# The second layer of a fused spectral filter and MLP as Strassen's seven products

## The chip, the cores and the metric

The kernel runs on one core of one Trainium2 chip. The metric is the time on the device in microseconds (us), the median of several runs. The core's engines work side by side, each in its own order: TensorE (PE, matmuls; its weight loads are shown as PEld), VectorE (DVE), ScalarE (ACT), GpSimd (POOL) and SyncE (SP, which here only starts DMAs). Matmul results land in PSUM; DVE and ACT carry them to SBUF.

## The reference

For 8 batches of 3008 tokens by 256 channels, a Fourier filter along the tokens, then two layers with a leaky ReLU between them over all 24064 tokens:

```python
X = np.fft.rfft(x, axis=1)
F = (filt_r + 1j * filt_i)[None, :, :]
y = np.fft.irfft(X * F, n=x.shape[1], axis=1)      # (8, 3008, 256)
h = y.reshape(24064, 256) @ w_in                   # 256 -> 2048
g = np.maximum(0.01 * h, h)
out = g @ w_out                                    # 2048 -> 256
```

Inputs and output are float32; the kernel works in float16 with float32 accumulation.

## The kernel before

**The two layers.** Tokens go in 47 chunks of 512 (CH). Time is cut into slots, eight to a chunk. In slot g of chunk ci, moe1_group (L397 to L415) computes layer one for two of the sixteen 128-wide blocks of the hidden dimension: four matmuls of 512 columns into one of two wide PSUM tiles (ph), then one ACT instruction that applies the leaky ReLU and writes 128x1024 float16 into the chunk's activation tile gts[ci]. In the same slot moe2_slice (L417 to L437) does an eighth of layer two of the chunk before: eight matmuls of 256 columns, with a 128x128 block of activations as the weights and a row block of w_out_sb as the moving operand. Two slots finish 128 tokens; ACT copies them from po_ps to an output buffer, and SP stores two such blocks at a time.

**The filter.** Each batch is filtered in two levels of a factored Fourier transform (94 x 32), as groups of matmuls with a turn through DRAM between them: s1_group (L195, 16 per batch), s2_group (L239, 12 per batch: two matmuls, then three DVE instructions L249 to L251 that multiply by the filter, and a POOL addition L253), sa_group (L257, 12 per batch), and sb_group (L267, 16 per batch), which writes the filtered tokens to yt. t1_load and t2_load bring the turned data back, x_load brings the next batch. Batch 0 is done ahead of the loop in another form. All groups take a PSUM tile from a ring of three (single, named pf) through bank(): a group's first matmul waits until the group three earlier has been copied out. The copies of s1_group and sa_group are ACT's (for batch 1 partly DVE's), those of sb_group are DVE's.

**The order.** The kernel writes its order by hand: every engine runs its instructions as the program lists them. plan() (L444) puts the groups of each batch into slots: for batch b from 2 on, 47b - 75 is the first slot of s1_group at 1.5 groups per slot, 47b - 60 that of s2_group with one every 2.5 slots, sa_group follows three slots later, and sb_group starts at 47b - 23 with 1.5 per slot. In a slot the order is layer one, then the planned groups, then the layer-two slice:

```python
    for slot in range(SL * (NCHUNK + 1)):
        ci, g = divmod(slot, SL)
        if ci < NCHUNK:
            moe1_group(ci, g)
        for f in tasks.get(slot, ()):
            f()
        if ci > 0:
            moe2_slice(ci - 1, g)
```

Of the kernel before, what the change touches and what calls it, by code (L numbers as in the profile page):

```python
# [10 lines left out]
P = 128  # L11
FP16 = mybir.dt.float16
FP32 = mybir.dt.float32
AL = mybir.AluOpType
# [58 lines left out]
def kernel(  # L73
# [9 lines left out]
    nc = tc.nc  # L83
    B, N, D = x.shape
    assert N == N1 * N2 and D == 256
    DFF = moe_w_in.shape[1]
    NCT = DFF // P
    NDT = D // P
    TOK = B * N
    CH = 512  # L90
    NCHUNK = TOK // CH
    assert NCHUNK * CH == TOK
    SL = 8

    f2_np, i1_np, small_np, f2t_np, i1t_np = _build_np_constants(N)
    f2_d = nc.inline_tensor(f2_np, name="fwd2_const")
# [10 lines left out]
    fb_sb = cpool.tile([P, NC, D], FP16, name="fb_sb")  # L107
    w_in_sb = cpool.tile([P, NDT, DFF], FP16, name="w_in_sb")
    w_out_sb = cpool.tile([P, NCT, D], FP16, name="w_out_sb")
    x_sb = cpool.tile([P, N2, D], FP16, name="x_sb")  # L110
    big = [cpool.tile([P, Q * D], FP16, name=f"big{i}") for i in range(3)]
    yt = cpool.tile([P, NDT, 2 * N], FP16, name="yt")
# [2 lines left out]
    drp = ctx.enter_context(tc.tile_pool(name="drp", bufs=1, space=bass.MemoryType.DRAM))  # L115
    scrp = ctx.enter_context(tc.tile_pool(name="scr", bufs=2))
    ypp = ctx.enter_context(tc.tile_pool(name="ypp", bufs=4))
    outp = ctx.enter_context(tc.tile_pool(name="outst", bufs=6))
    psp = ctx.enter_context(tc.tile_pool(name="psp", bufs=1, space=bass.MemoryType.PSUM))


    wide = [psp.tile([P, 2 * CH], FP32, name=f"ph{i}") for i in range(2)]
    single = [psp.tile([P, CH], FP32, name=f"pf{i}") for i in range(3)]
    po_ps = psp.tile([P, 2, D], FP32, name="po_ps")
    turn = {"ph": 0, "pf": 0}

# [44 lines left out]
    one = cpool.tile([1, 1], FP32, name="one")  # L171
# [6 lines left out]
    K4 = 4 * NC  # L178
# [16 lines left out]
    def s1_group(b, g, copy):  # L195
        def go():
            ps = bank("pf", 2, D)
            nc.tensor.matmul(ps, fwd1[:N1], x_sb[:N1, ds(2 * g, 2), :], start=True, stop=True)  # L198
            h = g // 2
            copy(st1[h % 4][:, ds(2 * (g % 2), 2), :], ps)  # L200
            if g % 2:
                nc.sync.dma_start(dz1[b % 2][ds(4 * h, 4)].rearrange("n p d -> p n d"), st1[h % 4])
        return go

    def t1_load(b, c):
        def go():
            nc.sync.dma_start(z1[c % 4], turned(dz1[b % 2], N2, c))
        return go

    def t2_load(b, h):  # L210
        def go():
            nc.sync.dma_start(z2[h % 4][:K4], turned(dz2[b % 2], NC, h))
        return go
# [25 lines left out]
    def s2_group(b, g):  # L239
        def go():  # L240
            ps = bank("pf", 2, D)
            for j in range(2):
                nc.tensor.matmul(ps[:, j, :], f2_sb[:, 2 * g + j, :],  # L243
                                 z1[g // 2 % 4][:, 2 * (g % 2) + j, :],
                                 start=True, stop=True)
# [3 lines left out]
            nc.vector.tensor_tensor(p1[:], ps, fa, AL.mult)  # L249
            nc.vector.scalar_tensor_tensor(p2[0:64], ps[64:P], -1.0, fb[64:P], AL.mult, AL.mult)  # L250
            nc.vector.tensor_tensor(p2[64:P], ps[0:64], fb[0:64], AL.mult)  # L251
            y1 = ypp.tile([P, 2, D], FP16, tag="y", name=f"y_b{b}_g{g}")
            nc.gpsimd.tensor_tensor(y1[:], p1[:], p2[:], AL.add)  # L253
            ys[(b, g)] = y1
        return go

    def sa_group(b, g):  # L257
        def go():
            ps = bank("pf", 2, D)
            nc.tensor.matmul(ps, inv2, ys.pop((b, g))[:], start=True, stop=True)  # L260
            h = g // 2
            nc.scalar.copy(st2[h % 4][:, ds(2 * (g % 2), 2), :], ps)  # L262
            if g % 2:
                nc.sync.dma_start(dz2[b % 2][ds(4 * h, 4)].rearrange("k p d -> p k d"), st2[h % 4])
        return go

    def sb_group(b, g, copy):  # L267
        h, dt = g // 2, g % 2

        def go():  # L270
            ps = bank("pf", 4, N1)
            for j in range(4):
                nc.tensor.matmul(ps[:, j, :], z2[h % 4][:K4, j, ts(dt, P)], i1_sb[:K4, 4 * h + j, :],  # L273
                                 start=True, stop=True)
# [6 lines left out]
    act, dve = nc.scalar.copy, nc.vector.tensor_copy  # L281
# [110 lines left out]
    nc.sync.dma_start(f2_sb[:], f2t_d.ap())  # L392


    gts, pos, osts = {}, {}, {}

    def moe1_group(ci, g):  # L397
# [16 lines left out]
                    )  # L414
        nc.scalar.activation(gts[ci][:, ds(2 * g, 2), :], ph, AF.Lrelu)  # L415

    def moe2_slice(ci, g):  # L417
        tj, half = g // 2, g % 2
        last = ci == NCHUNK - 1
        if last and half == 0:  # L420
            pos[ci] = bank("pf", 1, D)[:, 0, :]
        po = pos[ci] if last else po_ps[:, tj % 2, :]
        for ct in range(8 * half, 8 * half + 8):
            nc.tensor.matmul(po, gts[ci][:, ct, ts(tj, P)], w_out_sb[:, ct, :],  # L424
                             start=(ct == 0), stop=(ct == NCT - 1))
        if half == 0:
            return
        if tj % 2 == 0:
            osts[ci] = outp.tile([P, 2, D], FP32, tag="ost", name=f"ost_c{ci}_t{tj}")
        ost, t0 = osts[ci], ci * CH + tj * P  # L430
        nc.scalar.copy(ost[:, tj % 2, :], po)  # L431
        if last:
            nc.sync.dma_start(out[ds(t0, P), :], ost[:, tj % 2, :])
        elif tj % 2 == 1:
            nc.sync.dma_start(
                out[ds(t0 - P, 2 * P), :].rearrange("(j t) d -> t j d", t=P), ost[:])


    tasks = {}

    def at(slot, f):
        tasks.setdefault(int(slot), []).append(f)

    def plan(b, s1, per, s2, step, lag, sb, rate):  # L444
        for g in range(16):
            at(s1 + g / per, s1_group(b, g, dve if b == 1 and g % 4 < 3 else act))
            if g % 2 and b + 1 < B:
                at(s1 + g / per + 2, lambda n0=2 * g - 2: x_load(b + 1, n0, 4))
        for c in range(4):
            at(s2 - 3, t1_load(b, c))  # L450
        for g in range(12):
            at(s2 + step * g, s2_group(b, g))
            if g % 2 and g < 4:
                at(s2 + step * g, t1_load(b, 4 + g // 2))
            at(s2 + lag + step * g, sa_group(b, g))
        for h in range(4):
            at(sb - 3, t2_load(b, h))
        for g in range(16):
            at(sb + g / rate, sb_group(b, g, dve))
            if g % 2 and g < 8:  # L460
                at(sb + g / rate, t2_load(b, 4 + g // 2))

    at(9, lambda: nc.sync.dma_start(i1_sb[:K4], i1t_d.ap()))
    plan(1, 0, 2, 12.5, 1, 3, 31, 2)
    for b in range(2, B):
        z = 47 * b
        plan(b, z - 75, 1.5, z - 60, 2.5, 3, z - 23, 1.5)

    for slot in range(SL * (NCHUNK + 1)):
        ci, g = divmod(slot, SL)  # L470
        if ci < NCHUNK:
            moe1_group(ci, g)
        for f in tasks.get(slot, ()):
            f()
        if ci > 0:
            moe2_slice(ci - 1, g)


# [28 lines left out]
```

## Time and profile before

| | |
|---|---|
| Median of 3 runs | 795.32 us (793.85 to 796.42) |
| The profiled execution's own time | 793.45 us |
| Its span in the trace | 791.7 us |
| Granted TensorE clock, mean | 0.998 of full speed |
| DMA | 92.48 MB, mean 117 GB/s |
| Second layer: matmuls of 128x256 | 3008, in po_ps and (last chunk) pf |
| First layer: leaky ReLU instructions | 376, mean 1024 ns |

In the profile a group line names the source line, engine and operation, the output and input tiles, their shapes, and the count; then the busy time and the mean length of one instruction; then how long the engine stood idle just before instructions of the group, and which instruction ended that wait. A line in order of time begins with the start in us from the span's start and the length of a run of equal instructions; a bracket at its end gives the idle time before it and what released it. The chain that ended last is followed back from the last instruction, and gives each engine's share of it.

### The profile page before, as it was taken

The numbers are of one execution on the slowest core, as the hardware profiler recorded it, in microseconds if no ns is written. First come the engines' busy times: TensorE is split into PE (matmuls) and PEld (weight loads), VectorE is DVE, ScalarE is ACT, GpSimd is POOL, SyncE is SP. The second block draws the span as 40 slices with busy tenths as digits, with TensorE's granted clock in tenths as the row PEclk, the third lists the DMA queues.
The fourth block names the chain that finished last, engine by engine and source line by source line (L and its number), as shares of the span: only waits on it lengthen the run. The fifth ranks groups of instructions, "written<-read, shape, count | busy, mean of one in ns | idle before, by whom it ended". The sixth has DMA issues, their size and how long they took to land.

```text
span 791.7 us, 13770 instructions
## 1 busy us (share of the span) xinstructions
PE 772.6 (98%) x5685; PEld 521.8 (66%) x5685; DVE 267.3 (34%) x408; ACT 553.4 (70%) x785; POOL 158.5 (20%) x171
## 2 busy tenths in 40 slices
PE   9888989999999999999999999999999999999998
PEld 4545556666676666666668666666667767666666
DVE  5837416441344224441344403443144423100000
ACT  4766866678677786777766787677867766666664
POOL 5624402221122211222112222222002210000000
PEclk9999999999999999999999999999999999999999
DMA  9994693218731295224932169212642232001111
GB/s 189 243 248 139 152 236 106 67 55 196 203 94 54 69 235 162 67 67 118 240 114 76 54 148 243 85 58 67 178 138 84 67 94 82 34 34 41 41 41 54
DMA packets 105422, 92.48 MB, mean 117 GB/s; under 512 B 12096, under 2 KB 88512, under 8 KB 105168
## 3 DMA queue, kind: packets, MB, share of 16 engines
q1 hardware_dynamic: 90496, 75.13, 30.1%
q0 software_dynamic: 14864, 16.49, 13.8%
q8 instruction: 44, 0.72, 0.4%
q14 instruction: 18, 0.15, 0.1%
HBM read 57.48 MB, written 50.33 MB: 136 GB/s over the span
## 4 chain that ended last, share of the span: by engine, by line
PE 92%; DMA 3%; DVE 2%; ACT 2%; issue 0%; DVEq 0%; SPq 0%; ACTq 0%
PE po_ps L424 40%; PE ph L410 39%; PE pf L198 3%; PE pf L273 2%; PE pf L243 2%; DMA dz<-big 2%; PE pf L260 2%; DMA big<-dz 1%; PE po_ps L348 1%; PE pf L424 1%; PE pf L320 1%; PE ph L299 1%; DVE big L233 0%; ACT gt_c L415 0%; ACT big L262 0%
## 5 line engine op out<-in xcount | busy, mean ns | idle before, releaser
L415 ACT ACTIVATE gt_c<-ph 128x1024 f16<-128x1024 f32 x376 | 384.7, 1024 | 203.6 <-PE ph L410 202.8
L410 PE MATMUL ph<-yt,w_in_sb 128*128 128x512 f16 (+3 forms) x1600 | 386.4, 366 | 0.3 <-DVE yt L340 0.3
L424 PE MATMUL po_ps<-w_out_sb,gt_c 128*128 128x256 f16 x2944 | 381.5, 272 | 0.0
L424 PEld LDWEIGHTS <-gt_c 128*128 128x128 f16 x3008 | 291.6, 98 | 87.9 <-issue 8.2
L410 PEld LDWEIGHTS <-w_in_sb 128*128 128x128 f16 x1600 | 154.4, 98 | 100.8 <-issue 4.3
L253 POOL TENSOR_TENSOR y_b_g<-p_b_g,p_b_g 128x512 f16<-128x512 f32 x84 | 106.4, 1267 | 355.1 <-DVE p_b_g L251 354.2
L276 DVE CAST yt<-pf 128x376 f16<-128x376 f32 x112 | 58.0, 546 | 210.9 <-PE pf L273 210.8
L249 DVE TENSOR_TENSOR p_b_g<-pf,fa_sb 128x512 f32<-128x512 f32 x84 | 58.0, 691 | 179.2 <-PE pf L243 170.3
L431 ACT COPY ost_c_t<-po_ps 128x256 f32<-128x256 f32 x184 | 69.5, 377 | 8.6 <-PE po_ps L424 7.0
L250 DVE SCALAR_TENSOR_TENSOR p_b_g<-pf,fb_sb 64x512 f32<-64x512 f32 x84 | 58.2, 692 | 1.1
L200 ACT CAST big<-pf 128x512 f16<-128x512 f32 x100 | 55.8, 590 | 3.9 <-DMA dz<-big 3.9
L251 DVE TENSOR_TENSOR p_b_g<-pf,fb_sb 64x512 f32<-64x512 f32 x84 | 57.4, 683 | 1.1
L142 POOL DMA_DIRECT2D x_sb<-in_x_dram x62 | 31.9, 517 | 121.0 <-PE pf L198 120.2
L262 ACT CAST big<-pf 128x512 f16<-128x512 f32 x84 | 48.8, 581 | 0.3 <-PE pf L260 0.3
L198 PE MATMUL pf<-x_sb,small_sb 94*128 94x512 f16 x112 | 37.3, 379 | 5.0 <-DVE big L200 2.9
L273 PEld LDWEIGHTS <-big 96*128 96x128 f16 x448 | 27.7, 98 | 20.8 <-DMA big<-dz 3.6
L273 PE MATMUL pf<-i_sb,big 96*128 96x94 f16 x448 | 31.8, 206 | 3.1 <-DMA big<-dz 3.1
L243 PE MATMUL pf<-big,f_sb 128*128 128x256 f16 x168 | 32.1, 272 | 2.0 <-DMA big<-dz 1.8
L260 PE MATMUL pf<-y_b_g,small_sb 128*128 128x512 f16 x84 | 31.9, 379 | 0.6 <-DVE p_b_g L251 0.6
L243 PEld LDWEIGHTS <-f_sb 128*128 128x128 f16 x168 | 15.9, 98 | 19.5 <-issue 3.0
L348 PE MATMUL po_ps<-idle 128*128 128x512 f16 x49 | 14.8, 450 | 1.2 <-DVE one L172 1.2
L198 PEld LDWEIGHTS <-small_sb 94*128 94x128 f16 x112 | 10.4, 98 | 8.1 <-issue 0.4
(52 smaller groups left out, 142.6 us busy)
## 6 DMA issues: line engine op xcount, KB each, us to landing
dz<-big SPq DMA_DIRECT2D x98, 256.0 KB, 3.2
out_dram<-ost_c_t SPq DMA_DIRECT2D x92, 256.0 KB, 2.2
big<-dz SPq DMA_DIRECT2D x42, 256.0 KB, 3.4
big<-dz SPq DMA_DIRECT2D x56, 192.0 KB, 4.9
x_sb<-in_x_dram POOLq DMA_DIRECT2D x41, 192.0 KB, 5.4
x_sb<-in_x_dram POOLq DMA_DIRECT2D x2, 768.0 KB, 10.0
w_in_sb<-in_moe_w_in_dram POOLq DMA_DIRECT2D x1, 1024.0 KB, 14.2
w_out_sb<-in_moe_w_out_dram POOLq DMA_DIRECT2D x1, 1024.0 KB, 12.5
```

The source lines that it names most:

```text
L198: nc.tensor.matmul(ps, fwd1[:N1], x_sb[:N1, ds(2 * g, 2), :], start=True, stop=True)
L243: nc.tensor.matmul(ps[:, j, :], f2_sb[:, 2 * g + j, :], z1[g // 2 % 4][:, 2 * (g % 2) + j, :], start=True, stop=True)
L249: nc.vector.tensor_tensor(p1[:], ps, fa, AL.mult)
L250: nc.vector.scalar_tensor_tensor(p2[0:64], ps[64:P], -1.0, fb[64:P], AL.mult, AL.mult)
L251: nc.vector.tensor_tensor(p2[64:P], ps[0:64], fb[0:64], AL.mult)
L253: nc.gpsimd.tensor_tensor(y1[:], p1[:], p2[:], AL.add)
L273: nc.tensor.matmul(ps[:, j, :], z2[h % 4][:K4, j, ts(dt, P)], i1_sb[:K4, 4 * h + j, :], start=True, stop=True)
L276: copy(yv[:, :, ds(4 * h, 4)], ps.rearrange("p c a -> p a c"))
L410: nc.tensor.matmul(ph[:, j, ds(o, ln)], w_in_sb[:, dt, ts(ct, P)], yt[:, dt, ds(lo, ln)], start=(dt == 0), stop=(dt == NDT - 1),)
L415: nc.scalar.activation(gts[ci][:, ds(2 * g, 2), :], ph, AF.Lrelu)
L424: nc.tensor.matmul(po, gts[ci][:, ct, ts(tj, P)], w_out_sb[:, ct, :], start=(ct == 0), stop=(ct == NCT - 1))
L431: nc.scalar.copy(ost[:, tj % 2, :], po)
```

## The change

For 44 of the 47 chunks (2 to 45) layer two becomes Strassen's scheme in Winograd's form. The activations of a chunk are cut in quarters a11, a12, a21, a22 (256 tokens by 1024 hidden each, as the first index counts tokens), and so is w_out (b11 to b22, 1024 by 128). Seven products of quarters replace eight:

- four combinations of w_out's quarters are made once, on POOL (wt);
- for each chunk DVE makes four combinations of activation quarters, each 128x2048 float16: s1, then a21 in place, s2 and s4 (act_sums, one at the end of each of slots 0 to 3);
- a product is 16 matmuls of 128 columns: two token blocks t by eight hidden blocks c. A chunk has seven, 112 matmuls or 14 in each slot, in this order: 0: a11 b11; 1: s4 b22 of the chunk before; 2: a12 b21; 3: s2 wt[1]; 4: a21 wt[2]; 5: a22 wt[3]; 6: s1 wt[0]. Product p is items 16p to 16p + 15 of the chunk, so it ends in slot p + 1 (product 6 with slot 7), at item 2p + 1 of that slot;
- ACT copies product 0 to t1; every other product is added to a partial sum by DVE, product 6 to two, so that seven DVE instructions of 128x256 replace four ACT copies. The sums go to output buffers, or to u2, u3, u4, which lie in float32 in the tile big[0], as do s1, s2 and s4.

Products alternate between two PSUM tiles, po_ps and the third tile of the FFT ring. The ring of the planned groups keeps two tiles. Output buffers go from six to four.

The plan moves: x_load of batch 2 later by 7.5 slots, s1_group to 47b - 75.5, s2_group to 47b - 60.25 with one every 2.75 slots, sb_group to 47b - 22 at 1.25 per slot; the copies of sb_group are now ACT's (for batch 1 half and half); the load of i1_sb goes from slot 9 to 18. Chunks 0, 1 and 46 keep whole-width matmuls (plain), 16 to each 128 tokens, with ACT copies.

```diff
+    NCH = NCT // 2
+    W0 = 2
...
+    wt_sb = cpool.tile([P, 4, NCH, P], FP16, name="wt_sb")
...
-    outp = ctx.enter_context(tc.tile_pool(name="outst", bufs=6))
+    outp = ctx.enter_context(tc.tile_pool(name="outst", bufs=4))
...
+    psp_last = single[-1]
...
+    single.pop()
+    out_banks = [t[:].rearrange("p (a t d) -> p a t d", a=2, t=2)
+                 for t in (psp_last, po_ps.rearrange("p a d -> p (a d)"))]
...
-    def moe2_slice(ci, g):
...
+    b11, b12 = w_out_sb[:, :NCH, :P], w_out_sb[:, :NCH, P:]
+    b21, b22 = w_out_sb[:, NCH:, :P], w_out_sb[:, NCH:, P:]
+    wt = [wt_sb[:, i] for i in range(4)]
+    for o, i0, i1 in ((wt[0], b12, b11), (wt[1], b22, wt[0]), (wt[2], b22, b12), (wt[3], b21, wt[1])):
+        nc.gpsimd.tensor_tensor(o, i0, i1, AL.subtract)
+
+    TH = CH // 2
+    sums = big[0][:, : 3 * NCH * TH].rearrange("p (i c t) -> p i c t", i=3, c=NCH)
+    s1, s2, s4 = (sums[:, i] for i in range(3))
...
+    def quarter(ci, i, j):
+        return gts[ci][:, ts(j, NCH), ts(i, TH)]
+
+    def act_sums(ci, step):
+        a11, a12, a21, a22 = (quarter(ci, i, j) for i in range(2) for j in range(2))
+        o, i0, i1, op = ((s1, a21, a22, AL.add), (a21, a11, a21, AL.subtract),
+                         (s2, s1, a11, AL.subtract), (s4, a12, s2, AL.subtract))[step]
+        nc.vector.tensor_tensor(o, i0, i1, op)
...
+    def product(ci, a, w, after):
+
+        po = out_banks[done["products"] % 2][:, 0]
+        done["products"] += 1
+
+        def one(t, c):
+            nc.tensor.matmul(po[:, t], a[:, c, ts(t, P)], w[:, c, :],
+                             start=(c == 0), stop=(c == NCH - 1))
+            if t == 1 and c == NCH - 1:
+                after(po)
+        return [lambda t=t, c=c: one(t, c) for t in range(2) for c in range(NCH)]
...
+    def added(*sums):
+
+        def after(po):
+            for o, with_ in sums:
+                nc.vector.tensor_tensor(o() if callable(o) else o, po, with_, AL.add)
+        return after
+
+    def last_product(ci):
+        def after(po):
+            added((half(ci, 0, 1), u4))(po)
+            store(ci, 0)
+        return product(ci, s4, b22, after)
+
+    def products(ci):
+        a11, a12, a21, a22 = (quarter(ci, i, j) for i in range(2) for j in range(2))
+
+        def after5(po):
+            added((half(ci, 1, 1), u3), (u4, u2))(po)
+            store(ci, 1)
+
+        items = product(ci, a11, b11, lambda po: nc.scalar.copy(t1, po))
+        if ci > W0:
+            items += last_product(ci - 1)
+        else:
+            done["products"] += 1
+            items += [lambda: None] * (2 * NCH)
+        items += product(ci, a12, b21, added((lambda: half(ci, 0, 0), t1)))
+        items += product(ci, s2, wt[1], added((u2, t1)))
+        items += product(ci, a21, wt[2], added((u3, u2)))
+        items += product(ci, a22, wt[3], added((lambda: half(ci, 1, 0), u3)))
+        items += product(ci, s1, wt[0], after5)
+        return items
...
-                at(s1 + g / per + 2, lambda n0=2 * g - 2: x_load(b + 1, n0, 4))
+                at(s1 + g / per + (2 if b > 1 else 9.5), lambda n0=2 * g - 2: x_load(b + 1, n0, 4))
...
-            at(sb + g / rate, sb_group(b, g, dve))
+            at(sb + g / rate, sb_group(b, g, dve if b == 1 and g % 2 else act))
...
-    at(9, lambda: nc.sync.dma_start(i1_sb[:K4], i1t_d.ap()))
+    at(18, lambda: nc.sync.dma_start(i1_sb[:K4], i1t_d.ap()))
...
-        plan(b, z - 75, 1.5, z - 60, 2.5, 3, z - 23, 1.5)
+        plan(b, z - 75.5, 1.5, z - 60.25, 2.75, 3, z - 22, 1.25)
+
+    items = []
     for slot in range(SL * (NCHUNK + 1)):
         ci, g = divmod(slot, SL)
+        wino = W0 <= ci - 1 < NCHUNK - 1
+        if g == 0 and ci > 0:
+            items = products(ci - 1) if wino else plain(ci - 1)
+            if ci == NCHUNK:
+                items = last_product(ci - 2) + items
         if ci < NCHUNK:
             moe1_group(ci, g)
         for f in tasks.get(slot, ()):
             f()
-        if ci > 0:
-            moe2_slice(ci - 1, g)
+        for f in items[len(items) * g // SL : len(items) * (g + 1) // SL]:
+            f()
+        if wino and g < 4:
+            act_sums(ci - 1, g)
```

In the changed kernel the planned groups' matmuls stand at L202 (stage one), L247, L264 and L277, the POOL addition at L257, the products at L461, the DVE additions at L476 and the activation sums at L447.

More of the change, by code (lines that the diff above doesn't have):

```diff
@@ L415, in moe1_group @@
         nc.scalar.activation(gts[ci][:, ds(2 * g, 2), :], ph, AF.Lrelu)
-    def moe2_slice(ci, g):
-        tj, half = g // 2, g % 2
+    b11, b12 = w_out_sb[:, :NCH, :P], w_out_sb[:, :NCH, P:]
[5 more added lines that the diff above has]
+    sums = big[0][:, : 3 * NCH * TH].rearrange("p (i c t) -> p i c t", i=3, c=NCH)
@@ new lines @@
+    s1, s2, s4 = (sums[:, i] for i in range(3))
+    part = [big[0][:, 3 * NCH * TH :].bitcast(FP32)[:, ts(i, TH)].rearrange("p (t d) -> p t d", t=2)
+            for i in range(4)]
+    t1, u2, u3, u4 = part
+    def quarter(ci, i, j):
[5 more added lines that the diff above has]
+        nc.vector.tensor_tensor(o, i0, i1, op)
@@ new lines, with store @@
+    done = {"products": 0}
+    def store(ci, i):
+        t0 = ci * CH + i * TH
+        nc.sync.dma_start(out[ds(t0, TH), :].rearrange("(j t) d -> t j d", t=P), osts[ci, i][:])
+    def product(ci, a, w, after):
[7 more added lines that the diff above has]
+        return [lambda t=t, c=c: one(t, c) for t in range(2) for c in range(NCH)]
@@ new lines, in half @@
+    def half(ci, i, k):
+        if (ci, i) not in osts:
+            osts[ci, i] = outp.tile([P, 2, D], FP32, tag="ost", name=f"ost_c{ci}_h{i}")
+        return osts[ci, i][:, :, ts(k, P)]
+    def added(*sums):
[8 more added lines that the diff above has]
+        return product(ci, s4, b22, after)
@@ L419, in moe2_slice, with plain, one @@
+    def plain(ci):
         last = ci == NCHUNK - 1
[L420 to L423, printed above, removed]
+        def one(tj, ct):
+            po = out_banks[tj % 2].rearrange("p a t d -> p (a t d)")[:, :D]
             nc.tensor.matmul(po, gts[ci][:, ct, ts(tj, P)], w_out_sb[:, ct, :],
                              start=(ct == 0), stop=(ct == NCT - 1))
-        if half == 0:
-            return
@@ L428, in moe2_slice @@
[L428 to L436, printed above, removed]
+            if ct < NCT - 1:
+                return
+            i, j = divmod(tj, 2)
@@ L439 @@
+            if j == 0:
+                osts[ci, i] = outp.tile([P, 2, D], FP32, tag="ost", name=f"ost_c{ci}_h{i}")
+            nc.scalar.copy(osts[ci, i][:, j, :], po)
+            if last:
+                nc.sync.dma_start(out[ds(ci * CH + tj * P, P), :], osts[ci, i][:, j, :])
+            elif j == 1:
+                store(ci, i)
+        return [lambda tj=tj, ct=ct: one(tj, ct) for tj in range(4) for ct in range(NCT)]
     tasks = {}
```

## The prediction

> **What bounds the kernel now.** I read the shares of busy time first, then the chain that ended last, then the costliest groups, then the order of time inside single slots. Shares and chain:
>
> ```profile
> PE 772.6 (98%) x5685; PEld 521.8 (66%) x5685; DVE 267.3 (34%) x408; ACT 553.4 (70%) x785; POOL 158.5 (20%) x171
> PE 92%; DMA 3%; DVE 2%; ACT 2%; issue 0%; DVEq 0%; SPq 0%; ACTq 0%
> PE po_ps L424 40%; PE ph L410 39%; PE pf L198 3%; PE pf L273 2%; PE pf L243 2%; DMA dz<-big 2%; PE pf L260 2%; DMA big<-dz 1%; PE po_ps L348 1%; PE pf L424 1%; PE pf L320 1%; PE ph L299 1%; DVE big L233 0%; ACT gt_c L415 0%; ACT big L262 0%
> ```
>
> TensorE is the bound nearly everywhere, split evenly over the two layers. VectorE is idle two thirds of the time. The groups that give my durations:
>
> ```profile
> L415 ACT ACTIVATE gt_c<-ph 128x1024 f16<-128x1024 f32 x376 | 384.7, 1024 | 203.6 <-PE ph L410 202.8
> L424 PE MATMUL po_ps<-w_out_sb,gt_c 128*128 128x256 f16 x2944 | 381.5, 272 | 0.0
> L253 POOL TENSOR_TENSOR y_b_g<-p_b_g,p_b_g 128x512 f16<-128x512 f32 x84 | 106.4, 1267 | 355.1 <-DVE p_b_g L251 354.2
> L249 DVE TENSOR_TENSOR p_b_g<-pf,fa_sb 128x512 f32<-128x512 f32 x84 | 58.0, 691 | 179.2 <-PE pf L243 170.3
> ```
>
> [...] the pitch has to come from runs in order of time (start, length, engine, count):
>
> ```profile
> 400.40 0.34 PE L273 MATMUL pf<-i_sb,big 96*128 96x94 f16 x4
> 400.80 1.03 PE L424 MATMUL po_ps<-w_out_sb,gt_c 128*128 128x256 f16 x8
> ```
>
> Eight of 256 columns: (1.03 - 0.27)/7 = 109 ns each. Four of 94 columns, each with a fresh weight load: (0.34 - 0.206)/3 = 45 ns. A straight line through the two puts 128 columns at 58 ns; the 128-column pieces of L410 that stand where a chunk crosses the end of yt start 56 ns apart in the trace. I take 56.
>
> One slot with four FFT groups (PE alone), and a stage-two block with its neighbour on POOL:
>
> ```profile
> 88.51 1.03 PE L410 MATMUL ph<-yt,w_in_sb 128*128 128x512 f16 x4
> 89.37 0.38 PE L260 MATMUL pf<-y_b_g,small_sb 128*128 128x512 f16 x1
> 89.86 0.38 PE L243 MATMUL pf<-big,f_sb 128*128 128x256 f16 x2
> 90.08 0.38 PE L198 MATMUL pf<-x_sb,small_sb 94*128 94x512 f16 x1
> 91.12 0.38 PE L198 MATMUL pf<-x_sb,small_sb 94*128 94x512 f16 x1 [0.67 <-ACT big L262]
> 91.34 1.04 PE L424 MATMUL po_ps<-w_out_sb,gt_c 128*128 128x256 f16 x8
> 92.21 1.03 PE L410 MATMUL ph<-yt,w_in_sb 128*128 128x512 f16 x4
> ```
>
> ```profile
> 87.71 0.69 DVE L249 TENSOR_TENSOR p_b_g<-pf,fa_sb 128x512 f32<-128x512 f32 x1 [1.37 <-PE pf L243]
> 88.42 0.69 DVE L250 SCALAR_TENSOR_TENSOR p_b_g<-pf,fb_sb 64x512 f32<-64x512 f32 x1
> 89.12 0.68 DVE L251 TENSOR_TENSOR p_b_g<-pf,fb_sb 64x512 f32<-64x512 f32 x1
> 89.96 1.26 POOL L253 TENSOR_TENSOR y_b_g<-p_b_g,p_b_g 128x512 f16<-128x512 f32 x1 [1.72 <-DVE p_b_g L251]
> ```
>
> With three tiles in the ring the fourth group had to wait until ACT had copied the first, 2.61 us after the slot began (91.12 - 88.51): ACT must run the slot's leaky ReLU (1.02) before that copy (0.58). This slot lasted 3.70 us against 2.60 by its matmuls, 1.10 lost. And a stage-two group occupies DVE for 2.09 us in one piece.
>
> **What the skill says.** (1) The Trainium skill, "TensorE: Matmul & The Clock Gate", "Back-to-back issue gap": about 81 ns for a matmul of 128 columns in a stream of load and matmul pairs, 56 alone. The 45 ns above, with a load each, speak for 56. (2) "VectorE: DVE Perf Modes", "The perf-mode tier table": a tensor_tensor with all operands 16-bit in SBUF makes two results a cycle, 2048 elements in 1224 ns; in fp32 2293. No such instruction is in this trace. (3) "SBUF — State Buffer", "Who interferes with whom": a VectorE instruction with two SBUF inputs and a GpSimd instruction that reads SBUF lock each other out for a whole instruction. L249 to L251 take one input from PSUM and show no such thing.
>
> **The change, part by part.**
>
> *Matmuls.* 44 of 47 chunks change. Per chunk 64 x 109 = 6.98 us goes, 112 x 56 = 6.27 comes: 0.70 less, **-31.0 us** in all. This is the whole gain on offer.
>
> *ACT.* 176 output copies (0.377) go, 44 copies to t1 and 104 yt copies (about 0.5, as L340 on ACT) come: +2 us in sum, and 8 x 1.02 + 0.4 per chunk leaves slack. A t1 copy behind two stage-one copies is late by some 0.3; with about seven such places, **+2**.
>
> *DVE, sum.* Adds: L249 extrapolated to 256 columns is 0.42 (0.44 with the step between instructions), seven per chunk. Activation sums: 1.24 with that step by (2), four per chunk. About 7.9 us per chunk, 346 in all, less 57 of yt copies: 267 becomes about 556. Not a bound by its sum, so what counts is when.
>
> *DVE, order.* A product's PSUM tile is reused by the product after next, whose first matmul waits for the add. Product p ends in slot p+1 and product p+2 starts in slot p+2 at item 2(p+2): the add must be out within one product. A stage-two block ahead of it is in the way. Call the slot of a stage-two group k (within its chunk), time from its first L243. DVE frees at 0.48 + 2.09 = 2.57 (0.48: 89.86 to DVE's 90.34 in the slot above), the add is out at 3.07. PE gets to the next product at 0.22 (L243) + 0.78 (14 items) + 0.86 (layer one: 89.37 - 88.51) + 0.112(k+1) = 1.87 + 0.112(k+1).
>  - k=3: 3.07 - 2.31 = 0.76; k=4: 0.64; k=5: 0.53; k=6: none, since two layer-one groups lie between.
>  - k=2: the sum s2 is queued behind that add, and the fourth product needs it: 3.07 + 1.24 - 2.20 = 2.1.
>  - k=1: a sum, an add and s2's sum follow the block: 2.57 + 1.24 + 0.44 + 1.24 + 0.06 = 5.55 against 0.22 + 2 x (0.78 + 0.86) + 0.34 = 3.85: 1.7. k=0, one more sum and one more slot: 6.79 - 5.50 = 1.3. k=7, two adds first: 7.67 - 7.15 = 0.5.
>
> The new plan puts 72 groups into changed chunks, at k=0..7: 9, 8, 10, 8, 9, 10, 8, 10. Sum 11.6 + 13.6 + 20.9 + 6.1 + 5.8 + 5.3 + 0 + 5.2 = **+68.5**; about 3 less for groups that stand in the next slot and lengthen it. Nothing gives these waits back: PE takes its matmuls in order.
>
> *Lock between DVE and POOL.* If (3) holds, the sum of DVE that follows an add finds L253 (1.27) running: k=2 loses 0.96 more, k=1 0.83, k=0 0.9, k=3 0.6, k=7 0.5: 34 us in all. Without it 0. No trace shows it and POOL is often first only by 0.1 us; I take half, **+17**, and keep both ends.
>
> *Chunks without FFT work.* DVE: two adds, two sums, then the add of the second product (ready at 4.62 from the chunk's start), then s2's sum: out at 6.36, needed at 6.14. 0.2 in some 15 chunks, **+3**.
>
> *Two ring tiles instead of three.* Now the third group of a slot waits for the first one's copy: 2.61 after the slot's start, 2.54 if it is a yt copy, when PE would be there at 1.22 to 1.30. Price 1.3, the size of the 1.10 seen above. For batches 2 to 7 the new plan has 15 slots with three groups and 5 with four (1.6 each, the fourth waits 0.3 more): 27.5. For batch 1, six more at 1.3, and slots 19, 21, 23 lose 2.2 instead of 1.1: 11. Together **+38.5**. Slots with three groups cost nothing in the trace, with three tiles.
>
> *At nothing:* the four weight differences on POOL (4 x 2.5 by L253's rate; the first y_b_g comes some 20 us into the loop, POOL idles 355 us; without cover 10 us). Later x_loads (one batch ahead). Stores: same bytes, but they sit in SP's queue waiting for a late DVE, ahead of turned loads issued three slots (5.2 us) early that take 3.4 to 4.9: at most some 2 us in a few places. Fewer output buffers: four against at most three in use.
>
> Sum against the profiled execution: 793.45 - 31.0 + 68.5 - 3 + 17 + 38.5 + 3 + 2 = 888.5 (its span 791.7 and 1.75 around it, unchanged). The median of the runs is 1.9 higher, so **890 us**.
>
> **Rivals.**
>  - *The matmul saving wins* (faster): PE's waits for DVE do not form, because a block delays an add by less than PE's way to the next product. It decides at about 1.9 us from L243 to a free bank; I have 3.07 from measured rows. For it: DVE has two thirds of its time free. Then 793 - 31 + few = about 770.
>  - *Sums at one element a cycle*, 2.28 each: three stand before the fourth product, +3.1 in each of 44 chunks, +136: about 1025. For it: nothing but the absent row.
>  - *Weight loads set the pitch*, 81 ns: 112 x 81 = 9.07, +92 on PE instead of -31; longer slots shrink the DVE waits to about 40: about 965. Against: 45 ns at 94 columns.
>
> **How the numbers follow.** Forecast 0.80, its own range 845 to 925: down to no lock and two thirds of the ring waits (793 - 31 + 65 + 26 + 5 = 858, and some of the blocks half hidden), up to the full lock (907) and late loads. Saving wins 0.08, one element a cycle 0.07, 81 ns 0.05. The range for 8 in 10, 842 to 930, leaves the three out. About 0.3% is what a measurement tells from no change: faster 0.08, same 0.02 (a near cancelling), slower 0.90.
>
> **What would show it.** L461 at 56 ns a step in unbroken runs; the sums at about 1.22 us; DVE's share near 60%; idle time of PE ahead of L461, released by DVE (some 80 us), and ahead of L202, L247, L264 and L277, released by ACT (some 40); sums of DVE stretched beyond 1.22 beside L257 on POOL if the lock is real; and the last eight chunks, free of FFT, shorter than before. If PE shows few waits for DVE, the order argument is wrong; if L461 runs at 80 ns, the first term is.

## The result and the profile after

The changed kernel takes 901.29 us (897.17 to 904.96, 4 runs) against 794.60 us (793.85 to 796.42, 4 runs) for the one before on the same chip: a ratio of 1.134, 95% interval 1.128 to 1.140. The forecast was 890, with a range of 842 to 930. The profiled execution took 904.96 us, its span is 903.2 us, and the granted TensorE clock is 0.964 on average, where it was 0.998.

Shares of busy time, the clock in 40 slices, and the chain that ended last:

```profile
PE 782.4 (87%) x7797; PEld 539.3 (60%) x7797; DVE 578.0 (64%) x788; ACT 554.8 (61%) x757; POOL 184.2 (20%) x175
PEclk9999899899999999999999999999999989999999
PE 16%; DVE 1%; ACT 0%; issue 0%; DVEq 0%
```

VectorE is busy for 64%, where the forecast had near 60%, and no engine is full: TensorE fell from 98% to 87%. The clock dips in three slices, which it did in none before. The chain accounts for 17% of the span and breaks off there, so it is no help for this kernel; the waits have to do.

The waits of TensorE that other engines end (engine, line, what released it: us in total, times, longest; PEld's waits overlap PE's, so the two are not added):

```profile
PEld L461 <- DVE big L447: 60.0, 23, 4.7
PE po_ps L461 <- DVE big L447: 30.0, 12, 4.5
PE pf L461 <- DVE big L447: 26.1, 11, 4.5
PE pf L247 <- ACT yt L280: 11.1, 10, 1.2
PE pf L202 <- ACT yt L280: 8.8, 10, 1.1
PE pf L202 <- ACT big L266: 7.5, 7, 1.2
PE pf L277 <- DMA big<-dz: 7.2, 4, 2.6
PE po_ps L461 <- DVE big L476: 5.2, 12, 0.5
```

Two families are large. A product waits for an activation sum (L447), 56 us in 23 places; and a group with one of the two ring tiles waits for ACT's copy, in steps of about 1.1 us. The third forecast family, a product that waits for the addition that frees its tile (L476), is there too, but small in each place. In a few places a group waits for the turned data from DRAM (big<-dz).

The costliest groups concerned:

```profile
L257 POOL TENSOR_TENSOR y_b_g<-p_b_g,p_b_g 128x512 f16<-128x512 f32 x84 | 124.0, 1477 | 472.6 <-DVE p_b_g L255 379.7
L447 DVE TENSOR_TENSOR big<-big,gt_c 128x2048 f16<-128x2048 f16 x44 | 67.9, 1544 | 0.0
L447 DVE TENSOR_TENSOR gt_c<-gt_c 128x2048 f16<-128x2048 f16 x44 | 63.4, 1441 | 1.5
L476 DVE TENSOR_TENSOR ost_c_h<-po_ps,big 128x256 f32<-128x256 f32 x87 | 36.8, 422 | 71.4 <-PE po_ps L461 66.3
```

The addition takes 422 ns (forecast 0.42). The four sums average 1378 to 1544 ns (the two longest are shown), not 1224, and POOL's addition went from 1267 to 1477 ns. In order of time, the case "stage-two group in slot 2":

```profile
165.83 0.38 PE L247 MATMUL pf<-big,f_sb 128*128 128x256 f16 x2
166.83 1.03 PE L418 MATMUL ph<-yt,w_in_sb 128*128 128x512 f16 x4
167.44 0.69 DVE L254 SCALAR_TENSOR_TENSOR p_b_g<-pf,fb_sb 64x512 f32<-64x512 f32 x1
167.69 0.50 PE L461 MATMUL po_ps<-w_out_sb,gt_c 128*128 128x128 f16 x6
168.15 0.68 DVE L255 TENSOR_TENSOR p_b_g<-pf,fb_sb 64x512 f32<-64x512 f32 x1
168.86 0.42 DVE L476 TENSOR_TENSOR ost_c_h<-pf,big 128x256 f32<-128x256 f32 x1
168.97 1.26 POOL L257 TENSOR_TENSOR y_b_g<-p_b_g,p_b_g 128x512 f16<-128x512 f32 x1 [4.49 <-DVE p_b_g L255]
169.20 2.12 DVE L447 TENSOR_TENSOR big<-big,gt_c 128x2048 f16<-128x2048 f16 x1
171.38 1.04 PE L461 MATMUL pf<-wt_sb,big 128*128 128x128 f16 x8 [3.19 <-DVE big L447]
172.21 1.91 PE L418 MATMUL ph<-yt,w_in_sb 128*128 128x512 f16 x4
```

The fourth product stands from about 168.2 until VectorE has finished the filter block, an addition, and s2's sum. That sum takes 2.12 us; POOL's L257, which reads SBUF, had started 0.23 us earlier (a run below shows that this is the reason). And once TensorE goes on, its layer-one matmuls take 1.91 us instead of 1.03: the clock has been halved. The columns of the next view are the stretch, its length, the busy time and count of PE, PEld, DVE, ACT, POOL, then the granted clock, the DMA share and GB/s:

```profile
170.00:173.40 3.40, 2.02 (x11) 1.29 (x12) 2.79 (x3) 0.00 (x0) 0.24 (x1) 0.53 0.22 77
173.40:176.80 3.40, 3.40 (x20) 2.21 (x19) 0.42 (x1) 1.02 (x1) 0.00 (x0) 0.50 0.00 0
176.80:180.30 3.50, 3.20 (x35) 2.22 (x34) 2.45 (x4) 2.44 (x3) 0.27 (x1) 0.97 0.01 2
```

After a wait of 3.19 us TensorE ran two windows, 6.8 us, at half speed. The forecast has no such term.

**The account by slots.** I measured each slot from its first layer-one matmul to the next slot's, and took off its own matmuls at their pitch, read from unbroken runs in the traces (216, 109, 56 and 44 ns for 512, 256, 128 and 94 columns). What is left is excess. Before, the slots last 740.8 us, 724.4 of matmuls and 16.5 of excess (9.3 in slots 0 to 23). After, they last 851.1, 692.6 and 158.5:

| us | forecast | measured |
|---|---|---|
| Matmuls | -31.0 | -31.8 |
| Fourth slots of chunks: s2's sum (43) | about 69, 15 of it lock | 61.8 |
| Fifth to seventh slots: tile not yet free | 17 | 17.7 |
| Ring of two: slots of 3 or 4 groups from slot 24 on (23), and slots 0 to 23 | 38.5 | 36.8 + 7.2 |
| Other slots, mainly at half clock (23) | none | 23.8 |
| The rest, less the 7.2 of before | 1 | -5.4 |

The measured column adds up to +110 (851.1 - 740.8). Of the 36.8 us, 8.0 are not waits for a ring tile: in four of these slots TensorE waits for turned data from DRAM.

### The profile page after: what moved, and what is told of

It reads as the page before. It is cut to its first block, busy times and chain, and to the rows that moved or that the text cites. A ratio compares the mean times of both kernels' runs of the same rounds, so it can differ in the third digit from the quotient of the medians.

```text
span 903.2 us, 18460 instructions
## 1 busy us (share of the span) xinstructions
PE 782.4 (87%) x7797; PEld 539.3 (60%) x7797; DVE 578.0 (64%) x788; ACT 554.8 (61%) x757; POOL 184.2 (20%) x175
## 5 line engine op out<-in xcount | busy, mean ns | idle before, releaser
L257 POOL TENSOR_TENSOR y_b_g<-p_b_g,p_b_g 128x512 f16<-128x512 f32 x84 | 124.0, 1477 | 472.6 <-DVE p_b_g L255 379.7
L461 PEld LDWEIGHTS <-gt_c 128*128 128x128 f16 x2816 | 182.7, 99 | 49.9 <-issue 18.8
L461 PEld LDWEIGHTS <-big 128*128 128x128 f16 x2112 | 138.1, 100 | 89.0 <-DVE big L447 60.0
L461 PE MATMUL po_ps<-wt_sb,big 128*128 128x128 f16 x704 | 55.9, 224 | 32.0 <-DVE big L447 30.0
L476 DVE TENSOR_TENSOR ost_c_h<-po_ps,big 128x256 f32<-128x256 f32 x87 | 36.8, 422 | 71.4 <-PE po_ps L461 66.3
L476 DVE TENSOR_TENSOR ost_c_h<-pf,big 128x256 f32<-128x256 f32 x89 | 37.6, 422 | 69.9 <-PE pf L461 56.0
L461 PE MATMUL pf<-wt_sb,big 128*128 128x128 f16 x704 | 58.0, 229 | 27.7 <-DVE big L447 26.1
L447 DVE TENSOR_TENSOR big<-big,gt_c 128x2048 f16<-128x2048 f16 x44 | 67.9, 1544 | 0.0
L447 DVE TENSOR_TENSOR gt_c<-gt_c 128x2048 f16<-128x2048 f16 x44 | 63.4, 1441 | 1.5
L447 DVE TENSOR_TENSOR big<-gt_c 128x2048 f16<-128x2048 f16 x44 | 60.9, 1383 | 0.3
L447 DVE TENSOR_TENSOR big<-gt_c,big 128x2048 f16<-128x2048 f16 x44 | 60.6, 1378 | 0.0
L461 PE MATMUL po_ps<-wt_sb,gt_c 128*128 128x128 f16 x704 | 55.9, 224 | 5.0 <-DVE big L476 3.2
L461 PE MATMUL pf<-wt_sb,gt_c 128*128 128x128 f16 x704 | 55.9, 224 | 3.6 <-DVE ost_c_h L476 1.9
L202 PE MATMUL pf<-x_sb,small_sb 94*128 94x512 f16 x112 | 39.8, 384 | 18.9 <-ACT yt L280 8.8
L461 PE MATMUL po_ps<-w_out_sb,gt_c 128*128 128x128 f16 x704 | 53.9, 219 | 0.0
```

What stands on the lines that cost most here:

```text
L447: nc.vector.tensor_tensor(o, i0, i1, op)
L461: nc.tensor.matmul(po[:, t], a[:, c, ts(t, P)], w[:, c, :], start=(c == 0), stop=(c == NCH - 1))
L476: nc.vector.tensor_tensor(o() if callable(o) else o, po, with_, AL.add)
```

## The experiments

Each run stands beside runs of the kernel before on the same chip; ratios are to those. "Half clock" is the time with a halved TensorE clock after the first 38 us of the trace: 1.5 us before, 62.6 us after. "Excess" is as above.

**The ring and the plan without the products.** All chunks keep whole-width layer two; the ring of two, the plan, the copies on ACT and four output buffers stay.

```diff
-        wino = W0 <= ci - 1 < NCHUNK - 1
+        wino = False
-            if ci == NCHUNK:
-                items = last_product(ci - 2) + items
```

> The changed plan, ACT's copies of sb_group and the ring of two tiles, but the second layer in whole-width matmuls with ACT copies in all 47 chunks: no products, no sums, no additions on DVE. If the ring of two costs what the sum gave (38.5 us, 42 by my reading of the slots of the changed kernel), this takes 830 to 845 us, with waits of 1.2 to 1.4 us in every slot of three or four groups and none in the fourth slot of a chunk. If the ring is harmless by itself and all waits come from DVE, it takes about 800.

832.31 us, ratio 1.046 (1.041 to 1.050), half clock 13.4 us. Slots of three or four groups have 32.4 us of excess, slots 0 to 23 have 18.1, and the fourth slots 0.1. TensorE's waits for the ring are much those of the changed kernel:

```profile
PE pf L247 <- ACT yt L280: 12.3, 11, 1.2
PE pf L202 <- ACT yt L280: 9.5, 10, 1.1
PE pf L202 <- ACT big L266: 7.6, 7, 1.2
```

So 37 us of the loss has nothing to do with the products' own work. This run changed the plan and moved copies to ACT as well; that the missing tile is what costs is shown by the runs below that give the groups three or four tiles under the same plan: slots 0 to 23 then have 4.0 to 4.8 us of excess, where the changed kernel has 16.5.

**The products without the sums.** s1, s2 and s4 are never computed and a21 stays as it is; the products read what lies there.

```diff
-        if wino and g < 4:
-            act_sums(ci - 1, g)
```

> The changed kernel with the four activation sums of each chunk left out (the products read stale sums, so the output is not the reference's). If what is queued ahead of s2's sum makes the fourth product wait, the waits in the fourth slot of a chunk (62 us) go and only the additions behind a stage-two block stay: about 830 to 845 us. If the waits only follow DVE's volume (sums are 253 of its 578 us), some 44% of the waits for DVE go: about 865.

829.13 us, 1.042 (1.037 to 1.047), half clock 14.0. Fourth slots fall from 61.8 to 8.6; ring slots (37.5) and fifth to seventh slots (15.9) stay. The sums, with the half clock that follows their waits, cost 72 us, more than twice the gain in matmuls, although VectorE has room for them.

**The lock.** POOL's addition becomes an instruction that only writes zeros; the filter's real and imaginary parts are so left unadded.

```diff
-            nc.gpsimd.tensor_tensor(y1[:], p1[:], p2[:], AL.add)
+            nc.gpsimd.memset(y1[:], 0.0)
```

> The addition of GpSimd at the end of a stage-two group is replaced by filling its output with zeros, which reads nothing (the filter's result is left out, the output is not the reference's). If sums of DVE and additions of GpSimd lock each other out, all 176 sums take 1.22 us (instead of 1.22 to 2.18) and the time falls by 20 to 30 us, to 870 to 880. If the longer sums have another cause, they stay longer and the time stays near 900.

852.89 us, 1.072 (1.067 to 1.076): 48 us less, more than the 20 to 30 expected. One of the four sums, first in the changed kernel, then here (count, then shortest, median and longest in ns, first and last start):

```profile
L447 DVE TENSOR_TENSOR big<-big,gt_c x44: 1207/1217/2119, 101.3 to 882.7; 128x2048 f16<-128x2048 f16 x44
```

```profile
L447 DVE TENSOR_TENSOR big<-big,gt_c x44: 1212/1215/1218, 98.9 to 831.3; 128x2048 f16<-128x2048 f16 x44
```

Without a POOL instruction that reads SBUF no sum exceeds 1226 ns; with it 53 of 176 take over 1300 and up to 2182. This is what the Trainium skill, "SBUF — State Buffer", "Who interferes with whom", describes, and the trace now agrees. All sums together take 214.3 us here and 252.9 in the changed kernel. The fourth slots lose 25.9 of their 61.8 us; the rest of the 48 fits the clock: half clock drops by some 45 us, to 17 (45 x 0.49 = 22; the rate is shown below).

**Three ring tiles again.** The products use the two halves of the one tile po_ps.

```diff
-    single.pop()
-    out_banks = [t[:].rearrange("p (a t d) -> p a t d", a=2, t=2)
-                 for t in (psp_last, po_ps.rearrange("p a d -> p (a d)"))]
+    out_banks = [po_ps[:, a].rearrange("p (t d) -> p t d", t=2) for a in range(2)]
```

> The changed kernel with the ring of three tiles given back: the products alternate between the two halves of po_ps. If the ring waits stand beside the DVE waits, they go (about 42 us, and some of the low-clock windows with them): 850 to 860 us, with slots of three groups at their matmuls' length. If PE only comes sooner to its next wait for DVE, most of it returns there: above 880.

1112.38 us, 1.398 (1.390 to 1.405), a clear miss. In order of time:

```profile
900.69 0.83 PE L459 MATMUL po_ps<-wt_sb,gt_c 128*128 128x128 f16 x12
901.56 0.42 DVE L474 TENSOR_TENSOR ost_c_h<-po_ps,big 128x256 f32<-128x256 f32 x1 [2.01 <-PE po_ps L459]
902.04 0.27 PE L459 MATMUL po_ps<-wt_sb,big 128*128 128x128 f16 x2 [0.52 <-DVE ost_c_h L474]
```

A product in one half starts only when VectorE has read the other half. TensorE's waits of this kind sum to 273 us (121.2 and 91.6 for VectorE, 59.8 for ACT). Whether the wait is one of the program's own order, which may be kept by tile, or one of the memory, this run doesn't tell. Before the change the halves alternated too, but layer one and the groups mostly lay between. On a ring of three this run shows only that slots 0 to 23, before the first product, have 4.6 us of excess instead of 16.5.

**The sums ahead of the planned groups.** VectorE gets s1 and a21's sum at the start of slot 0, s2's in slot 1, s4's in slot 3.

```diff
         if ci < NCHUNK:
             moe1_group(ci, g)
+        for step in {0: (0, 1), 1: (2,), 3: (3,)}.get(g, ()) if wino else ():
+            act_sums(ci - 1, step)
         for f in tasks.get(slot, ()):
...
-        if wino and g < 4:
-            act_sums(ci - 1, g)
```

> The changed kernel with the same instructions, but the sums stand ahead of the slot's planned groups: s1 and a21 at the start of slot 0, s2 in slot 1, s4 in slot 3. No work is removed. If the waits come from the order in DVE's queue, s2's sum no longer stands behind a stage-two block of slots 1 and 2; by the same arithmetic the blocks then cost about 45 us instead of the 80 that the slots of the changed kernel show, the lock with GpSimd little, and with fewer low-clock windows the time is 835 to 855 us. If the volume of DVE's work is what counts, it stays near 900.

874.81 us, 1.099 (1.092 to 1.106), half clock 42.8. It helps, but misses: fourth slots fall only to 34.6, and fifth to seventh rise to 24.2. VectorE's own order shows why:

```profile
145.06 1.79 DVE L447 TENSOR_TENSOR big<-gt_c 128x2048 f16<-128x2048 f16 x1
146.89 1.22 DVE L447 TENSOR_TENSOR gt_c<-gt_c 128x2048 f16<-128x2048 f16 x1
148.03 1.22 DVE L447 TENSOR_TENSOR big<-big,gt_c 128x2048 f16<-128x2048 f16 x1
149.16 0.68 DVE L253 TENSOR_TENSOR p_b_g<-pf,fa_sb 128x512 f32<-128x512 f32 x1
149.86 0.69 DVE L254 SCALAR_TENSOR_TENSOR p_b_g<-pf,fb_sb 64x512 f32<-64x512 f32 x1
150.57 0.68 DVE L255 TENSOR_TENSOR p_b_g<-pf,fb_sb 64x512 f32<-64x512 f32 x1
151.28 0.42 DVE L476 TENSOR_TENSOR ost_c_h<-po_ps,big 128x256 f32<-128x256 f32 x1
151.76 0.61 PE L461 MATMUL po_ps<-wt_sb,big 128*128 128x128 f16 x8 [2.25 <-DVE ost_c_h L476]
```

s2 is in time, but now the filter block stands after three sums in a row, and the addition that frees a tile is late behind it: TensorE waits 2.25 us for that instead. The queue was reordered and no shorter.

**The groups spread thinner.** Stage one at one group per slot, stage two moved.

```diff
+    plan(2, 24, 2, 37, 2.5, 3, 72, 1)
-        plan(b, z - 75.5, 1.5, z - 60.25, 2.75, 3, z - 22, 1.25)
+        plan(b, z - 75.5, 1, z - 56.5, 2.5, 3, z - 22, 1)
```

> The changed kernel with another plan alone: one group of stage one and of the inverse stage per slot, stage two from 47b - 56.5 with one every 2.5 slots, batch 2 by numbers of its own, so that 14 slots hold three or four groups instead of 29; the stage-two groups fall on the slots of a chunk as evenly as before. If a ring wait is paid for every such slot, some 20 us go with a little low clock: 865 to 882. If DVE's waits grow by what the ring gives back, about 900.

879.44 us, 1.105 (1.100 to 1.109): as expected. Slots of three or four groups, now 14, have 18.7 us of excess, and slots 0 to 23 have 7.0. The plan alone gets back a fifth of the loss.

**One ring of four tiles for groups and products.** A group takes the tile used longest ago that no running product holds; a product keeps its tile until its last matmul.

```diff
+    def take(hold=False):
+        t = next(r for r in rota if not any(r is h for h in held))
+        rota.remove(t)
+        rota.append(t)
+        if hold:
+            held.append(t)
+        return t
```

> The changed kernel with the four single PSUM tiles in one ring for products and planned groups (the tile used longest ago is next; the one of an unfinished product is passed over). If reuse of a tile is the cause of the ring waits (42 us) and of the waits for additions (18), both go, and the waits for s2's sum (62) stay: 820 to 840 us. If only the first-come order matters and tiles are no limit: about 895.

900.81 us, 1.132 (1.125 to 1.138): nothing. Slots 0 to 23 fall to 4.0 us of excess, but slots of three or four groups keep 36.3. "Used longest ago" was counted from a product's first matmul. A product fills its tile over 16 matmuls, more than a slot's worth. Where three groups ran meanwhile, its tile was the oldest when it ended, and the next product or group was given the one just filled, which VectorE had yet to empty; where two ran, the one after next was. In the program's order the first falls to 14 products and 5 groups, the second to 38 and 42; with the ring counted from the end, below, the three other tiles are always handed out first.

The same ring with the sums first and the thinner plan:

> Sums first, the shared ring of four and the other plan together. If the three causes are the whole loss, what is left of the sum is the matmuls' gain (-31), about 10 us of waits for s2's sum where a stage-two block falls into slot 0, and some 10 us around batches 1 and 2: 775 to 790 us, less than both kernels. If a fourth cause is at work (a low clock of its own, loads turned late), above 800.

863.78 us, 1.083 (1.078 to 1.088): missed and inconclusive, since it has the same flaw.

**The ring counted from the end.** The flaw mended: when a product ends, its tile goes to the end of the ring.

```diff
+    def free():
+        t = held.pop()
+        rota[:] = [r for r in rota if r is not t] + [t]
```

> The changed kernel with the shared ring of four, in which a product's tile goes to the end of the ring when the product is finished, not when it begins. In the first shared ring (e9) a product often got the very tile that the product before it had just filled, and waited for its addition at once. If reuse of tiles is the cause of the ring waits and of the additions' waits, they go now and the waits for s2's sum (62 us) with their low clock stay: 820 to 845 us. If tiles are no limit, 895 again.

851.68 us, 1.071 (1.061 to 1.080), a little beyond the range expected. Slots 0 to 23 have 4.8 us of excess, fifth to seventh slots 1.9, slots of three or four groups 21.2 (8.7 of it waits for turned data from DRAM). The fourth slots keep 61.0: a larger ring doesn't touch the wait for the sums.

```profile
PEld L477 <- DVE big L461: 58.4, 25, 4.7
PE pf L477 <- DVE big L461: 45.8, 20, 4.5
```

(L461 is the sums' line in this kernel, L477 the products'.)

**This ring and the sums first.** s1 and a21 at the start of slot 0, s2 at that of slot 1, s4 after slot 2; the plan is the changed kernel's.

```diff
+        for step in {0: (0, 1), 1: (2,)}.get(g, ()) if wino else ():
+            act_sums(ci - 1, step)
...
-        if wino and g < 4:
-            act_sums(ci - 1, g)
+        if wino and g == 2:
+            act_sums(ci - 1, 3)
```

> The shared ring by end and the activation sums ahead of the planned groups together, with the plan of the changed kernel: e11 and the order of e12, without e12's places for stage two. Theory: the two causes are separate, so the fourth slots' 61.0 us of e11 fall to about 30, as they fell when only the sums were moved (34.6), and the slots of three groups stay near 21: 851.7 - 30 and some 8 us less of half clock = 805 to 830, and e12's last 35 to 50 us belong to the places of stage two. Rival: the ring and the sums' order account for nearly all of e12 (at most 790), and the places for nothing.

816.49 us, 1.026 (1.022 to 1.030), inside the range of the first theory. The fourth slots fall from 61.0 to 12.1, more than expected, and half clock from 54.0 to 9.4; slots of three or four groups have 18.4, fifth to seventh 19.7.

**And the stage-two groups where VectorE is free.** From batch 2 on, they stand in slots 3, 5 and 7 of four chunks, and sb_group moves with them.

```diff
+        def when(g):
+            return s2 + step * g if b == 1 else s2 + SL * (g // 3) + 2 * (g % 3)
...
-        plan(b, z - 75.5, 1.5, z - 60.25, 2.75, 3, z - 22, 1.25)
+        c0 = SL * ((z - 56) // SL)
+        plan(b, z - 75.5, 1.5, c0 + 3, 0, 3, c0 + 39, 1.25)
```

> This ring, the sums of slots 0 and 1 ahead of the planned groups (s4's after slot 2), and the stage-two groups of batches 2 to 7 put into slots 3, 5 and 7 of a chunk, behind s2's sum. If the order on DVE and the reuse of tiles are the whole loss, the matmuls' gain shows: 770 to 795 us, with hardly a low-clock window after the first batches. If the products cost something by themselves that these do not reach, above 800.

778.92 us (778.01 to 782.79) against 796.14: 0.981 (0.977 to 0.985), faster than both kernels. The page, and one form of a product:

```profile
PE 748.5 (96%) x7797; PEld 524.4 (68%) x7797; DVE 551.5 (71%) x788; ACT 551.5 (71%) x757; POOL 167.9 (22%) x175
L477 PE MATMUL pf<-wt_sb,big 128*128 128x128 f16 x1040 | 80.0, 220 | 1.2 <-ACT yt L296 1.1
```

Fourth slots 0.1 us, fifth to seventh 6.1, slots of three or four groups (21) 13.3, slots 0 to 23 4.6, half clock 8.1. VectorE does every instruction of the changed kernel. The three edits to order and allocation in a row give 901.3, 851.7, 816.5, 778.9. The slots last 725.1 us in all, 15.7 less than before the change: 31.8 us fewer of matmuls, and some 16 us more of excess. That the gain is the products', and not that of the new ring and places, rests on this account; the whole-width second layer with this ring and these places was not run.

**The clock.** The changed kernel, with 20 needless matmuls ahead of the fourth product in the chunks with a stage-two group in slots 0 to 2 (in the program 25, not the 27 of the expectation: 500 matmuls); the product's first true matmul overwrites them.

```diff
+            if filled is not None and t == c == 0:
+                for _ in range(20):
+                    nc.tensor.matmul(po[:, 0], filled[:, 0, :P], b11[:, 0, :],
+                                     start=True, stop=True)
```

> The changed kernel, with 20 needless matmuls of 128 columns (1.12 us) into the product's own tile ahead of the fourth product, in the 27 chunks with a stage-two group in slots 0 to 2; the product's first true matmul overwrites them. They stand where TensorE waits for s2's sum anyway (1.0 to 5.1 us a chunk), after the addition that frees the tile. Theory: half clock follows a window in which matmuls stream for less than about 0.4 of the time, and it costs some 0.49 us per us: the half-clock time after the first 38 us falls from 62.6 us to 10 to 30, and the kernel gets 10 to 25 us faster by doing more work: 875 to 892. Rival: half clock only fills time in which TensorE waits for VectorE anyway, or does not come from the waits: 898 to 910.

893.73 us (890.08 to 897.73), 1.123 (1.117 to 1.128) against the change's 1.134 (1.128 to 1.140): 7.6 us less at the median for 500 more matmuls, just outside the range expected, and small against the spread of the runs. The trace is clearer. Half clock falls from 62.6 to 37.4 us (10 to 30 were expected), and the slots put down as mainly at half clock have 7.1 us of excess instead of 23.8, with 14.5 us at half clock instead of 48.8: 0.49 us per us both times. About half of this gain doesn't show in the time. Two of the 25 places had no wait for s2's sum, and there the filler costs its whole 1.1 us. Slots 0 to 23 lost 3.5 us more, with twice the half clock, and one slot of four groups 3.7, since TensorE waited there 3.3 us for turned data instead of 0.7; no filler stands in either, and nothing of the edit comes before slot 24, so the first of these is a difference between two executions.

## Why the prediction was right, and where it was not

The forecast of 890 us is 1.3% low. Its mechanism is what the runs show: VectorE's queue and the PSUM tiles, not VectorE's volume, make TensorE wait. Part of the closeness of the number is luck, since errors of opposite sign cancel, in the sum and inside one of its terms.

- **Matmuls: right.** -31.8 against -31.0. The pitch shows in an unbroken run of twelve: (0.83 - 0.219)/11 = 55.5 ns, with a weight load each (0.219 us: the mean of one).

```profile
840.75 0.83 PE L461 MATMUL po_ps<-w_out_sb,big 128*128 128x128 f16 x12
```

 So the rival "81 ns" is out, and the figure of the Trainium skill, "TensorE: Matmul & The Clock Gate", "Back-to-back issue gap", for load and matmul pairs is not met here.
- **DVE, order: the mechanism right, the prices too high.** Waits stand where the sum put them. Fifth to seventh slots: 17.7 against 17.2. By the place k of the stage-two group, the fourth slot's excess was 1.0 to 1.7 us at k=0 (forecast 1.3, before the lock), 2.0 to 3.0 at k=1 (1.7; nothing in one chunk whose second slot had already lost 2.9 us to the ring), 2.8 to 3.7 at k=2 (2.1), about 5 where a chunk had groups at 0 and 2. k=7, for which I had 0.5, shows 0.03 where it stands alone (the chunk after one with groups at 1, 4 and 7). Fourth slots without a group in slots 0 to 2 have 0.16 at most. These figures contain the lock. In the run with POOL only writing, the excess is at most 0.7 at k=0, 0.7 to 1.6 at k=1 and 1.9 to 2.0 at k=2: all fourth slots together 36 us, where the sum has 54 before the lock (k=0, 1, 2 and 7, and the chunks without FFT work).
- **Lock: nearly the full price, not half of it.** The sums behind a filter block at k=2 lose 0.90 us (2.12 against 1.22), close to the full 0.96, and without POOL's reads the fourth slots lose 25.9 us. I had 15 for them, 29 at the full price, 5 of it for k=7, where no wait came. The lock some 11 us too low, the waits before it some 18 too high: the row of the table is near its forecast because the two cancel, which is luck.
- **Chunks without FFT work: too much.** In the last seven chunks the excess is 0.3 us in all; a slot takes 1.645 us, where it took 1.736 before. There the change does what its arithmetic says.
- **Ring of two: right, and late loads too low.** 44.0 us against 38.5, of which 8.0 us stood at half clock (about 4 us by the rate above) and 8.0 us are waits for turned data from DRAM in four slots. For such loads I had "at most some 2 us in a few places"; the ring itself is some 36 us or less. Apart from these four, slots of three groups lost 1.24 to 1.33 us each, of four 1.30 to 1.44. The run without products shows the cost alone, +37 us.
- **What was missing: the clock.** 62.6 us at half clock, at 0.49 each, are at most some 30 us of the loss (an estimate: the filler run showed 0.49 in the slots concerned, and where TensorE waits anyway half clock costs less). My waits of 2 to 5 us were listed as lost time and nothing else; that they slow what comes after them is no step of the sum. Against the profiled execution the sum is 16.5 us low (904.96 against 888.5). By the same estimate that is some 30 for the clock that it left out, less some 14 by which its other terms were too high together: without their own half clock, the fourth slots were 9 too high and the rest 7, the ring row 2 too low.
- **The rivals.** "The matmul saving wins" decides, I wrote, at 1.9 us from L247 to a free tile; the trace has 3.4 (a group's first matmul at 165.83, the addition out at 169.28). "One element a cycle" falls with sums of 1.21 to 1.23 us wherever POOL is not in the way.

## What to carry to other kernels

An engine with two thirds of its time free can still be what another one waits for: add up what stands in its queue ahead of the instruction that frees a tile or delivers an operand, for each place where a block may fall. Algorithmic savings on the bound engine are paid in buffers and in order; here the same products and sums lose 13% or gain 2% only by who takes which PSUM tile and by where the sums and the filter's groups stand. And a ring of buffers that are held for different times must count from the end of use.

## What the runs showed of the hardware

**A wait can halve the clock without TensorE being idle throughout.** The Trainium skill, "TensorE: Matmul & The Clock Gate", "What's actually happening", has the clock halved after an idle window of about 3.4 us, on a grid of 3413 ns. The grid is there: all half-clock stretches in the traces last 3.413 or 6.827 us, apart from a last one that the end of the trace cuts off. But a whole idle window is not needed. I cut the trace of the changed kernel into windows of the grid, and took for each the share in which matmuls streamed (a matmul from its start to the next one's, at most its length less 160 ns, by which a matmul of 512 or 256 columns outlasts its pitch). Of the windows at full clock after 38 us, all 16 with a share up to 0.38 were followed by a halved one, and none of the 217 from 0.43 upward. In the filler run it is 9 of 9 up to 0.38 and none of 230 from 0.40; in the kernel before the lowest share is 0.46 and nothing is halved. The border isn't sharp: over the traces of all the runs here, all 103 windows up to 0.36 were followed by a halved one, 19 of the 61 between 0.36 and 0.47, and none of the 3079 above. So waits of about 2.1 us inside one window were enough, at a cost of 3.4 us at half speed or more.

**Halves of one PSUM tile gave no overlap** between TensorE's writes and the reads of VectorE and ACT (273 us of waits, 1112 us against 901), at least as this program orders them.
